# First pass of a batch in two steps of groups instead of three, and room for stacked tiles asked for later

## The chip, the cores and the metric

The kernel runs on one core of one Trainium2 chip. The metric is the device time of one execution in microseconds (us). Five engines work side by side, each through its own instructions in order: TensorE (PE, with its weight loads shown apart as PEld), VectorE (DVE), ScalarE (ACT), GpSimd (POOL) and SyncE (SP), which here only issues DMA transfers. They wait for one another by semaphores. A difference of about 0.2% (3 us) is what a measurement of this kernel can tell from no change.

## The reference, cut to what matters

```python
B, N, m, C = (4, 12480, 32, 128)
def mab(q, kv):
    s = scale * (q @ kv.transpose(0, 2, 1))
    s = s - s.max(-1, keepdims=True)
    a = np.exp(s)
    a /= a.sum(-1, keepdims=True) + 1e-09
    return a @ kv
h = mab(I, x)                       # 32 inducing rows look at the 12480 rows of a batch
x = mab(x, h).reshape(B * N, C)     # every row looks at the 32 rows of h
h = x @ w_in                        # 128 -> 2048
g = np.maximum(0.01 * h, h)
return g @ w_out                    # 2048 -> 128
```

All of it is float32. A batch therefore has a **first pass** (scores of the inducing rows against all rows, a softmax along 12480, the product with the rows: h), a **second pass** (scores of every row against h, a softmax along 32) and the two layers after it.

## The kernel before, in words

The last two layers are most of the work. The rows of all batches make 98 tiles, nearly all of 512 columns, and a tile goes through 16 **units**, one for each 128 of the 2048: 1568 units in all. A unit is four TensorE products of 512 columns and two evacuations: `ph` (line 712, the first layer, into PSUM), then on ACT `ghi` (line 725, the rectified value rounded to a short format) and on DVE `glo` (line 733, what the rounding left), then three products into `po` (line 751: ghi with w_hi, glo with w_hi, ghi with w_lo). At a tile's last unit one product more is added (line 770), and later DVE turns `po` into `osb` (line 780), which SP stores.

The products are written three units ahead (`LOOK = 3`): `ph` of unit u + 3 stands ahead of the `po` products of unit u. `ph` comes from the PSUM pool `ps_h`, which has three buffers. Helpers of the attention borrow from the same pool by `gen_ps`; other PSUM pools are `aux_ps` (two buffers), `ps_s` (one, tag `hp`) and `ps_o` (two, for `po`).

The attention of the next batch is woven into this stream. A loop over the units calls a few generators ("lanes"), and each call writes the next piece: `stores`, `stacking`, `seconds` (the softmax of the second pass for one group of rows), `scores` (`first_scores`) and `values` (`first_values`, then the weights for the next batch). A piece that costs DVE some 0.7 us yields `HEAVY` = 15; this debt is paid off by 4 a unit (5 in batch 0), and while there is debt the other lanes wait. So such pieces stand four units apart (three in batch 0).

The rows of a batch are 6 groups of 2048 and a remainder `RG` of 192. The first pass takes them in steps (`PASSES`) with a running maximum. At each step `first_scores` writes one **visit** of TensorE to the attention: the products of the step before with the rows (`value_products`), up to two second scores that the batch before still has to do (`waiting`, PSUM by `gen_ps`, each followed by its transpose on DVE, `turned`), and the first scores of the step's groups. Then `peaks` copies each group's scores out of PSUM into `e` on DVE and takes their maximum (line 282, called a peak below); it is the only reader of that PSUM buffer. One more visit brings the last value products, another the second scores that `expand_weights` starts with.

```python
ps_h = ctx.enter_context(tc.tile_pool(name="ps_h", bufs=LOOK, space=bass.MemoryType.PSUM))
def gen_ps(name):
    return ps_h.tile([P, TOK], F32, tag="ph", name=name)
```

`stack` makes the tiles `A4` that line 712 multiplies: ACT splits off `ahi` (line 641), POOL `alo` (line 646), both with one buffer, and SP copies them by DMA into `A4` (line 658), of which there are six.

Batch 0 has its first pass in an order written out by hand (`ORDER`), which the change does not touch; the weaving holds for the first passes of batches 1 to 3.

Of the kernel before, what the change touches and what calls it, by code (L numbers as in the profile page):

```python
# [20 lines left out]
def induced_attention_then_leaky_ffn(  # L21
# [24 lines left out]
    P = 128  # L46
# [81 lines left out]
    ring = set()  # L128
    PASSES = [[RG, 0, 1], [2, 3], [4, 5]]
    PASS_OF = {g: p for p, gs in enumerate(PASSES) for g in gs}  # L130
# [71 lines left out]
    def room(n=1):  # L202

        return not rows_live or rows_made[0] + n - 1 - min(i for i, _ in rows_live) < XR

# [63 lines left out]
    def peaks(b, p, sps):  # L269

        gs = PASSES[p]
        rm = sb.tile([P, len(gs)], F32, tag="rm", name="rm", bufs=2)
        if RG in gs:
            nc.vector.memset(rm[:, :1], -3.0e38)
        for i, g in enumerate(gs):
            _, J, K = GROUPS[g]
            w, rows = 32 * K, 32 * J
            if g == RG:
                e = sb.tile([P, w], F32, tag="er", name="er", bufs=1)
            else:  # L280
                e = sb.tile([P, TOK], F32, tag="e", name="e", bufs=2)
            nc.vector.tensor_scalar(  # L282
                out=e[:rows, :w],
                in0=sps[g][:rows, :w],
                scalar1=1.0,
                scalar2=None,
                op0=ALU.mult,
                op1=ALU.max,
                accum_out=rm[:rows, i : i + 1],
            )  # L290
            ex[b, g] = e
        return rm

    def running(b, p, rm):
        gs = PASSES[p]
        n = len(gs)
        nm_old = maxima.get(b)
        zg = sb.tile([P, 3], F32, tag="zg", name="zg", bufs=2)
# [3 lines left out]
        four = sb.tile([M, 12], F32, tag="rd", name="four", bufs=2)  # L302
        al = None
        for j in range(4):
            nc.gpsimd.tensor_scalar_mul(four[:, n * j : n * j + n], rm[32 * j : 32 * j + 32], -SCALE)
        yield
        if nm_old is None:
            nc.vector.tensor_reduce(out=nm[:M], in_=four[:, : 4 * n], op=ALU.min, axis=AX.X)
        else:
            least = sb.tile([M, 12], F32, tag="least", name="least", bufs=2)  # L310
# [12 lines left out]
        for i, g in enumerate(gs):  # L323
            _, J, K = GROUPS[g]
            w, rows = 32 * K, 32 * J
            e = ex[b, g]
            nc.scalar.activation(
                e[:rows, :w], e[:rows, :w], AF.Exp, bias=nm[:rows], scale=SCALE,
                accum_out=zg[:rows, i : i + 1],
            )  # L330
            yield
        zs = sb.tile([P, 1], F32, tag="zs", name="zs", bufs=2)
        nc.vector.tensor_reduce(out=zs, in_=zg[:, :n], op=ALU.add, axis=AX.X)
        if al is not None:
# [27 lines left out]
    def first_scores(b):  # L362


        halves = [(RG, 0, 3)] + [(g, j0, 2) for g in range(RG) for j0 in (0, 2)]
        blocks = {}
# [9 lines left out]
        for p, gs in enumerate(PASSES):  # L376
# [85 lines left out]
    def first_values(b):  # L462

        hacc = None
        for p, gs in enumerate(PASSES):
            while (b, p) not in summed:
                yield
            for g in gs:
# [3 lines left out]
                if g == RG:  # L472
                    ay = sb.tile([P, K, M], F32, tag="ayr", name="ayr", bufs=1)
                else:
                    ay = sb.tile([P, 16, M], F32, tag="ay", name="ay", bufs=2)
                nc.vector.transpose(ay[:rows, :K, :].rearrange("p k m -> p (k m)"), e[:rows, : 32 * K])
# [30 lines left out]
    def normalise(b, hacc, rz):  # L507

        same = e128.rearrange("p j m -> p (j m)")
        hs = sb.tile([P, C], F32, tag="hs", name="hs", bufs=1)  # L510
        nc.scalar.mul(hs, hacc, rz)
# [21 lines left out]
    def expand_weights(b):  # L533
# [4 lines left out]
        if b:  # L538
            while not room(2):
# [37 lines left out]
    def second(b, g, engines=None):  # L577
# [4 lines left out]
        rows, w = 32 * J, 32 * K  # L582
        if b == B - 1 and (b, g) not in early and g != RG and g > 1:
            while hw[b][2] is None or not room(len(waiting)):
# [43 lines left out]
    def stack(tiles_, engine=None):  # L628

        while len(A4) + len(tiles_) > A4_BUFS or not all(s[:2] in aT for t in tiles_ for s in t[1]):  # L630
            yield
# [11 lines left out]
        for (b, g), o in at.items():  # L643
# [192 lines left out]
    def start(stacking, seconds, chosen):  # L836
# [57 lines left out]
        def peak(g):  # L894
# [5 lines left out]
            if g == RG:  # L900
                e = sb.tile([P, TOK], F32, tag="e", name="e", bufs=2)
            else:
# [62 lines left out]
        def Y(g):  # L965
            J, K, rows, w = size(g)
            V["ay", g] = ay = sb.tile([P, 16, M], F32, tag="ay", name="ay", bufs=2)
            nc.vector.transpose(
# [35 lines left out]
        def gather(p):  # L1004
            hp = V.pop(("hp", p))[:, :C]
            if p == len(STEPS) - 1:
                V["hs"] = new = sb.tile([P, C], F32, tag="hs", name="hs", bufs=1)
                nc.vector.scalar_tensor_tensor(
# [20 lines left out]
        def scaled():  # L1029
            V["samez"] = r = sb.tile([P, P], F32, tag="samez", name="samez", bufs=1)  # L1030
            nc.scalar.mul(r, same, V["rz"])
# [76 lines left out]
        def first_second():  # L1108
# [3 lines left out]
            yield  # L1112
            y = sb.tile([P, 16, M], F32, tag="y", name="y", bufs=1)
            chosen["ysub"].tensor_tensor(
# [23 lines left out]
        def scales():  # L1138
            apart = sb.tile([P, 4, 16], F32, tag="apart", name="apart", bufs=1)
            nc.vector.tensor_tensor(  # L1140
# [10 lines left out]
        def scales_copy():  # L1151
            r = sb.tile([P, 4, 16], F32, tag="scr", name="scr", bufs=1)
            nc.scalar.copy(r.rearrange("p t k -> p (t k)"), V.pop("sc")[:, :64])
            token_scale.append(r)
# [45 lines left out]
        def second_turned(g):  # L1200
# [3 lines left out]
            if g:  # L1204
                y = sb.tile([P, 16, M], F32, tag="y", name="y", bufs=1)
                nc.vector.transpose(y.rearrange("p k m -> p (k m)"), V.pop(("s2", g)))
# [90 lines left out]
    with tc.manual_schedule():  # L1297
# [12 lines left out]
        for u in range(WOVEN, NT * NF):  # L1310
# [12 lines left out]
            if u >= 52 and u % 2:  # L1323
                step(fetches)
            if not debt[0]:
                step(seconds)
            if u >= max(due[0], 52) and not debt[0]:
                due[0] = u + (2 if b or u % 4 else 1)
                step(scores)
            if u >= 52 and (u >= due[1] or hw[max(hw)][2] is None) and not debt[0]:  # L1330
                due[1] = u + (2 if b or u % 4 else 1)
                known = len(hw)
                step(values)
                if len(hw) > known:
                    seconds += [second(known, g) for g in [0, 1, RG, 2, 3, 4, 5]]
        for gen in stores:
# [35 lines left out]
```

## Time and profile before

| what | value |
|---|---|
| median of 3 runs | 1491.11 us (1490.77 to 1491.75) |
| the profiled execution | 1490.82 us, span 1488.6 us |
| TensorE busy | 1477.5 us (99% of the span) |
| VectorE busy | 1262.6 us (85%) |
| ScalarE busy | 999.7 us (67%) |
| GpSimd busy | 116.7 us (8%) |
| granted TensorE clock | 0.999 |

The span runs from the first to the last instruction of the program; 2.2 us of the execution lie around it. The profile's matmul ends are modelled, and consecutive matmuls overlap in it, so the time of a stream is read from start to start.

### The profile page before, as it was taken

To read this page: it belongs to the slowest core of one execution; us is meant where nothing else is said; L and a number is where in the kernel's file an instruction comes from. 1 tells how busy PE (TensorE), PEld (TensorE's weight loads), DVE (VectorE), ACT (ScalarE), POOL (GpSimd) and SP (SyncE) were. 2 spreads that over 40 slices of the span, in tenths; PEclk is the share of its full clock that TensorE was granted. 3 is DMA by queue.
4 is the path that set the end of the run, shared out by engine and by line. 5 is a ranking of instruction groups with operands and counts; after the bars stand their busy time and mean duration, and the time that the engine had idled before them with its cause. 6 is when DMAs were issued, how large, how long until landed. Compare 5 with 4: busy or idle time off the path is not lost.

```text
span 1488.6 us, 22239 instructions
## 1 busy us (share of the span) xinstructions
PE 1477.5 (99%) x7861; PEld 1260.5 (85%) x7861; DVE 1262.6 (85%) x2129; ACT 999.7 (67%) x1749; POOL 116.7 (8%) x186
## 2 busy tenths in 40 slices
PE   9999999999999999999999999999999999999998
PEld 6788888888888888888888888888888898888887
DVE  6889889889898898889898898788888888888886
ACT  6766767666665766667675776676776666666665
POOL 1310101010100100010100100010100000000000
PEclk9999999999999999999999999999999999999999
DMA  8336355435444342343443440231212212212211
GB/s 286 67 81 119 53 89 118 93 66 97 92 89 82 95 92 51 55 89 67 91 88 69 110 92 16 48 71 21 46 36 40 43 22 50 43 22 50 40 25 22
DMA packets 402079, 105.23 MB, mean 71 GB/s; under 512 B 372624, under 2 KB 375088, under 8 KB 401968
## 3 DMA queue, kind: packets, MB, share of 16 engines
q1 hardware_dynamic: 401920, 103.80, 34.5%
q8 instruction: 62, 1.02, 0.3%
q14 instruction: 49, 0.40, 0.1%
q10 hardware_dynamic: 48, 0.02, 0.0%
HBM read 48.94 MB, written 25.56 MB: 50 GB/s over the span
## 4 chain that ended last, share of the span: by engine, by line
PE 98%; DMA 1%; DVE 0%; ACT 0%; issue 0%; SPq 0%; DVEq 0%; ACTq 0%
PE po L751 68%; PE ph L712 23%; PE s_ps L264 3%; PE po L770 1%; PE h_ps L440 1%; PE xT_ps L874 1%; DMA xr<-in_x_dram 0%; PE h_ps L995 0%; PE hw_ps L547 0%; PE w_ps L1095 0%; ACT ghi L725 0%; DMA hws<-hilo 0%; SPq L846 0%; PE winT_ps L1085 0%; DVE osb L780 0%
## 5 line engine op out<-in xcount | busy, mean ns | idle before, releaser
L725 ACT ACTIVATE ghi<-ph 128x512 fp32r<-128x512 f32 (+1 forms) x1568 | 929.3, 595 | 461.9 <-PE ph L712 456.3
L733 DVE SCALAR_TENSOR_TENSOR glo<-ph,ghi 128x512 fp32r<-128x512 f32 (+1 forms) x1568 | 1042.8, 679 | 183.0 <-ACT ghi L725 161.3
L712 PE MATMUL ph<-A,hws 128*128 128x512 f32 (+1 forms) x1600 | 594.9, 377 | 0.4 <-DMA hws<-hilo 0.3
L751 PE MATMUL po<-glo,w_hi 128*128 128x512 f32 (+1 forms) x1568 | 593.1, 378 | 1.2 <-DVE glo L733 1.2
L751 PE MATMUL po<-ghi,w_lo 128*128 128x512 f32 (+1 forms) x1568 | 593.0, 378 | 0.0
L751 PE MATMUL po<-ghi,w_hi 128*128 128x512 f32 (+1 forms) x1568 | 592.8, 379 | 0.0
L712 PEld LDWEIGHTS ph<-A,hws 128*128 128x128 f32 x1600 | 301.9, 189 | 58.1 <-DVE e L282 5.0
L751 PEld LDWEIGHTS po<-glo,w_hi 128*128 128x128 f32 x1568 | 296.4, 189 | 42.7 <-DVE glo L733 1.6
L751 PEld LDWEIGHTS po<-ghi,w_lo 128*128 128x128 f32 x1568 | 296.3, 189 | 41.2
L751 PEld LDWEIGHTS po<-ghi,w_hi 128*128 128x128 f32 x1568 | 296.4, 189 | 39.9 <-ACT ghi L725 0.2
L780 DVE STREAM_TRANSPOSE osb<-po 128x512 f32<-128x512 f32 (+1 forms) x98 | 68.9, 703 | 1.5 <-PE po L770 1.5
L646 POOL TENSOR_TENSOR alo<-aT,ahi 128x512 fp32r<-128x512 f32 x22 | 28.2, 1282 | 483.1 <-ACT ahi L641 463.2
L397 DVE STREAM_TRANSPOSE xT<-xc 128x512 f32<-128x512 f32 x72 | 50.5, 701 | 0.0
L599 POOL TENSOR_TENSOR y<-y,mx 128x512 f32<-128x512 f32 x23 | 24.2, 1052 | 243.6 <-DVE mx L597 219.1
L614 POOL TENSOR_TENSOR y<-y,sm 128x512 f32<-128x512 f32 x23 | 24.2, 1052 | 196.9 <-DVE sm L612 145.5
L770 PE MATMUL po<-A,m2s 128*128 128x512 f32 (+1 forms) x100 | 37.1, 374 | 0.0
L357 DVE STREAM_TRANSPOSE y<-s_ps 128x512 f32<-128x512 f32 x22 | 15.8, 717 | 10.9 <-PE s_ps L264 9.3
L264 PE MATMUL s_ps<-xT,hT 128*32 128x512 f32 x192 | 23.8, 596 | 0.4 <-ACT hT L1039 0.4
L264 PE MATMUL s_ps<-xT,indT 128*32 128x512 f32 x192 | 24.1, 595 | 0.0
L770 PEld LDWEIGHTS po<-A,m2s 128*128 128x128 f32 x100 | 18.9, 189 | 2.6
L282 DVE TENSOR_SCALAR_CACHE_REDUCE e<-s_ps 128x512 f32<-128x512 f32 x18 | 12.4, 690 | 8.0 <-PE s_ps L264 7.2
L440 PEld LDWEIGHTS h_ps<-xr,ay 128*32 128x32 f32 x576 | 15.2, 110 | 2.9 <-issue 2.6
(165 smaller groups left out, 376.1 us busy)
## 6 DMA issues: line engine op xcount, KB each, us to landing
xr<-in_x_dram SPq DMA_DIRECT2D x96, 256.0 KB, 4.4
out_dram<-osb SPq DMA_DIRECT2D x384, 64.0 KB, 2.2
xc<-in_x_dram SPq DMA_DIRECT2D x288, 64.0 KB, 2.8
A<-ahi SPq DMA_DIRECT2D x188, 64.0 KB, 2.0
A<-alo SPq DMA_DIRECT2D x188, 64.0 KB, 2.0
hws<-hilo SPq DMA_DIRECT2D x64, 64.0 KB, 2.0
raw<-in_moe_w_in_dram SPq DMA_DIRECT2D x4, 512.0 KB, 6.8
raw<-in_moe_w_out_dram SPq DMA_DIRECT2D x4, 512.0 KB, 10.3
```

The costliest lines, as they stand in the source:

```text
L264: nc.tensor.matmul(dst, lhsT, rhs, start=True, stop=True)
L397: nc.vector.transpose(t[:, j, :], blk.rearrange("p n c -> p (n c)"))
L440: nc.tensor.matmul(hp[32 * k : 32 * k + 32, :C], ay[:rows, 4 * q + k, :], xb[:rows, k, :], start=(i == 0 and q == 0), stop=(last[k] == i a ...
L599: engines[0].tensor_tensor(out=yv, in0=yv, in1=mx[:rows, :K].unsqueeze(2).broadcast_to([rows, K, M]), op=ALU.subtract,)
L614: engines[1].tensor_tensor(out=yv, in0=yv, in1=smv.unsqueeze(2).broadcast_to([rows, K, M]), op=ALU.mult)
L646: (engine or nc.gpsimd).tensor_tensor(out=alo[sl], in0=aT.pop((b, g))[: 32 * J, :], in1=ahi[sl].bitcast(F32), op=ALU.subtract,)
L712: nc.tensor.matmul(ph[:, o : o + w], hw[b][1][:, f * P : (f + 1) * P], woven(A4[t][:, o : o + w], t), start=True, stop=True,)
L725: nc.scalar.activation(halves(ghi[:, :n], t)[1], live[u][2], AF.Relu)
L733: nc.vector.scalar_tensor_tensor(out=halves(glo[:, :n], t)[1], in0=ph, scalar=0.0, in1=halves(ghi[:, :n], t)[1].bitcast(F32), op0=ALU.max, ...
L751: nc.tensor.matmul(accs[t][:, :n], w[:, f, :], woven(r[:, :n], t), start=(f == 0 and w is w_hi and r is live[u][0]), stop=False,)
L770: nc.tensor.matmul(accs[t][:, o : o + w], hw[b][2], woven(a4[:, o : o + w], t), start=False, stop=(o + w == n),)
L780: nc.vector.transpose(osb[:, :n], po[:, :n])
```

## The change

The first pass of batches 1 to 3 has two steps, groups 0, 1, 2 and then RG, 3, 4, 5. Their scores now lie in `aux_ps`, `aux_ps` and `hp` in the first step, and in `gen_ps` (RG), `aux_ps`, `aux_ps`, `gen_ps` (group 5) in the second. `peaks` yields `HEAVY` behind each group but the last. All waiting second scores (three now, since `expand_weights` does four groups itself) are written at once. The wait of `stack` for free `A4` buffers stands behind `ahi` and `alo`. The lanes that are called in a unit stop at the first debt, and `values` comes first while the next batch's weights are missing. Several SBUF tiles share tags, so that `e` and `ay` have three buffers.

```diff
-    PASSES = [[RG, 0, 1], [2, 3], [4, 5]]
+    PASSES = [[0, 1, 2], [RG, 3, 4, 5]]
...
-        return not rows_live or rows_made[0] + n - 1 - min(i for i, _ in rows_live) < XR
+        return len(rows_live) + n <= XR
...
-                e = sb.tile([P, TOK], F32, tag="e", name="e", bufs=2)
+                e = sb.tile([P, TOK], F32, tag="e", name="e", bufs=3)
...
             ex[b, g] = e
+            if i + 1 < len(gs):
+                yield HEAVY if g != RG else 0
         return rm
...
-            while b - 1 not in hw or hw[b - 1][2] is None or not room(min(2, len(waiting))):
+            while b - 1 not in hw or hw[b - 1][2] is None or not room(len(waiting)):
                 yield
...
-            for q in [waiting.pop(0) for _ in range(min(2, len(waiting)))]:
+            for q in [waiting.pop(0) for _ in range(len(waiting))]:
                 ps = gen_ps("s2_ps")
...
-                if g == RG:
+                if g == 2:
                     sps[g] = ps_s.tile([P, TOK], F32, tag="hp", name="s1_ps")
+                elif g in (RG, 5):
+                    sps[g] = gen_ps("s1_ps")
                 else:
                     sps[g] = aux_ps("s1_ps")
...
-            rm = peaks(b, p, sps)
+            rm = yield from peaks(b, p, sps)
...
-            for g, ps in [(RG, gen_ps("s2_ps")), (0, aux_ps("s2_ps")), (1, ps_s.tile([P, TOK], F32, tag="hp", name="s2_ps"))]:
+            for g in (RG, 2, 0, 1):
+                if g == 1:
+                    ps = ps_s.tile([P, TOK], F32, tag="hp", name="s2_ps")
+                else:
+                    ps = aux_ps("s2_ps") if g == 0 else gen_ps("s2_ps")
                 second_scores(b, g, ps)
                 turned(b, g, ps)
-            waiting.extend(range(2, RG))
+            waiting.extend(range(3, RG))
...
-        while len(A4) + len(tiles_) > A4_BUFS or not all(s[:2] in aT for t in tiles_ for s in t[1]):
+        while not all(s[:2] in aT for t in tiles_ for s in t[1]):
             yield
...
         yield
+        while len(A4) + len(tiles_) > A4_BUFS:
+            yield
         for t, parts in tiles_:
...
-            if not debt[0]:
-                step(seconds)
-            if u >= max(due[0], 52) and not debt[0]:
+            urgent = hw[max(hw)][2] is None
+            for lane in (values, seconds, scores) if urgent else (seconds, scores, values):
+                if debt[0]:
+                    break
```

TensorE carries out the same matmuls before and now. What moves is best seen at the visit of the second step of batch 1. On TensorE before, the visit ends with one second score (`s2_ps`, from `gen_ps`) and the first scores of groups 2 and 3 (`s1_ps`, both from `aux_ps`):

```order
L440 MATMUL h_ps_2960<-xr_1438,ayr_2420 32x128 x2
L264 MATMUL s2_ps_2995<-xT_409,hT_653 32x512 x4
L264 MATMUL s1_ps_3002<-xT_2443,indT_82 32x512 x4
L264 MATMUL s1_ps_3007<-xT_2674,indT_82 32x512 x4
L712 MATMUL ph_3017<-A4_1975,hws_675 128x512
L751 MATMUL po_2867<-ghi_2935,w_hi_79 128x512
```

On TensorE now it ends with RG (`s1_ps_3549`, from `gen_ps`), groups 3 and 4 (`aux_ps`) and group 5 (`s1_ps_3563`, from `gen_ps`):

```order
L444 MATMUL h_ps_3500<-xr_1945,ay_3453 32x128 x4
L264 MATMUL s1_ps_3549<-xTr_2697,indT_82 32x64 x3
L264 MATMUL s1_ps_3553<-xT_2773,indT_82 32x512 x4
L264 MATMUL s1_ps_3558<-xT_3003,indT_82 32x512 x4
L264 MATMUL s1_ps_3563<-xT_3223,indT_82 32x512 x4
L722 MATMUL ph_3574<-A4_2691,hws_675 128x512
L761 MATMUL po_3372<-ghi_3475,w_hi_79 128x512
```

So two buffers of the pool of `ph` are taken by first scores, which before had none of that pool.

On DVE before, at the same place, the transpose of the second score and both peaks follow one another between two `glo`:

```order
L733 SCALAR_TENSOR_TENSOR glo_2955<-ph_2951,ghi_2953 128x512
L357 STREAM_TRANSPOSE y_3000<-s2_ps_2995 128x512
L282 TENSOR_SCALAR e_3013,rm_3012<-s1_ps_3002 128x512
L282 TENSOR_SCALAR e_3015,rm_3012<-s1_ps_3007 128x512
L733 SCALAR_TENSOR_TENSOR glo_3021<-ph_3017,ghi_3019 128x512
```

On DVE now the peaks of RG and group 3 stand first, two `glo` apart; three `glo` on come the peak of group 4 and what follows here, up to that of group 5:

```order
L282 TENSOR_SCALAR e_3625,rm_3568<-s1_ps_3558 128x512
L743 SCALAR_TENSOR_TENSOR glo_3631<-ph_3627,ghi_3629 128x512
L743 SCALAR_TENSOR_TENSOR glo_3642<-ph_3638,ghi_3640 128x512
L743 SCALAR_TENSOR_TENSOR glo_3654<-ph_3650,ghi_3652 128x512
L790 STREAM_TRANSPOSE osb_3659<-po_3372 128x512
L743 SCALAR_TENSOR_TENSOR glo_3666<-ph_3662,ghi_3664 128x512
L743 SCALAR_TENSOR_TENSOR glo_3675<-ph_3671,ghi_3673 128x512
L743 SCALAR_TENSOR_TENSOR glo_3686<-ph_3682,ghi_3684 128x512
L282 TENSOR_SCALAR e_3695,rm_3568<-s1_ps_3563 128x512
L743 SCALAR_TENSOR_TENSOR glo_3701<-ph_3697,ghi_3699 128x512
```

From the visit to the peak of group 5, the only reader of `s1_ps_3563`, there are now 11 `glo`; in batch 2 there are 26 and in batch 3 there are 17. The other DVE instructions of the 0.7 us kind ahead of that last peak are: in batch 1 two peaks and one `osb`; in batch 2 two peaks, two `osb`, one `aT` and one `mx`; in batch 3 two peaks, one `osb` and one `aT`.

On ACT the splits for the tile that batches 0 and 1 share (`ahi<-aTr`, twice) are followed by the next split after 19 `ghi` now:

```order
L649 CAST ahi<-aTr 96x64 x2
L735 ACTIVATE ghi<-ph 128x512 x3
L329 ACTIVATE e,zg<-e,nm 128x512
L735 ACTIVATE ghi<-ph 128x512 x5
L329 ACTIVATE e,zg<-e,nm 128x512
L735 ACTIVATE ghi<-ph 128x512 x9
L613 ACTIVATE y<-y 128x512
L735 ACTIVATE ghi<-ph 128x512 x2
L649 CAST ahi<-aT 128x512
```

Before, 59 `ghi` stood between the two.

## Rows read from the trace of the kernel before

**Rows 1.** The page: busy us by engine, and the chain that ended last.
```profile
PE 1477.5 (99%) x7861; PEld 1260.5 (85%) x7861; DVE 1262.6 (85%) x2129; ACT 999.7 (67%) x1749; POOL 116.7 (8%) x186
...
PE 98%; DMA 1%; DVE 0%; ACT 0%; issue 0%; SPq 0%; DVEq 0%; ACTq 0%
```

**Rows 2.** The view of waits, PE alone: us in total, times, longest.
```profile
PE po L751 <- DVE glo L733: 1.2, 1, 1.2
...
PE ph L712 <- DMA hws<-hilo: 0.3, 1, 0.3
```

**Rows 3.** Busy us by stretch: PE, PEld, DVE, ACT, POOL; then clock, DMA.
```profile
0.00:50.00 50.00, 46.10 (x482) 31.46 (x483) 35.76 (x100) 33.21 (x67) 9.95 (x13) 1.00 0.70 230
...
446.00:600.00 154.00, 154.00 (x892) 132.88 (x895) 132.93 (x226) 102.40 (x182) 11.51 (x25) 1.00 0.38 78
```

**Rows 4.** Timeline at 432 us, plain units: start, us, engine, instruction [idle before].
```profile
432.65 0.38 PE L712 MATMUL ph<-A,hws 128*128 128x512 f32 x1
...
433.06 0.60 ACT L725 ACTIVATE ghi<-ph 128x512 fp32r<-128x512 f32 x1 [0.27 <-PE ph L712]
...
433.51 0.38 PE L712 MATMUL ph<-A,hws 128*128 128x512 f32 x1
...
433.69 0.69 DVE L733 SCALAR_TENSOR_TENSOR glo<-ph,ghi 128x512 fp32r<-128x512 f32 x1 [0.17 <-ACT ghi L725]
...
434.30 0.68 DVE L609 TENSOR_REDUCE sm<-y 128x16 f32<-128x512 f32 x1
...
434.89 0.70 DVE L397 STREAM_TRANSPOSE xT<-xc 128x512 f32<-128x512 f32 x1
...
435.52 2.55 DVE L733 SCALAR_TENSOR_TENSOR glo<-ph,ghi 128x512 fp32r<-128x512 f32 x4
...
435.89 0.38 PE L751 MATMUL po<-ghi,w_lo 128*128 128x512 f32 x1
436.23 0.19 PEld L712 LDWEIGHTS ph<-A,hws 128*128 128x128 f32 x1 [0.37 <-DVE glo L733]
...
436.55 0.38 PE L751 MATMUL po<-ghi,w_hi 128*128 128x512 f32 x1
...
436.75 0.60 ACT L725 ACTIVATE ghi<-ph 128x512 fp32r<-128x512 f32 x1 [0.50 <-PE ph L712]
```

**Rows 5.** Timeline at 383 us: the visit of the first step of batch 2.
```profile
383.42 0.69 DVE L733 SCALAR_TENSOR_TENSOR glo<-ph,ghi 128x512 fp32r<-128x512 f32 x1 [0.17 <-ACT ghi L725]
...
383.88 0.38 PE L751 MATMUL po<-ghi,w_lo 128*128 128x512 f32 x1
...
384.19 0.16 PEld L264 LDWEIGHTS s_ps<-xT,hT 128*32 128x32 f32 x8 [0.33 <-DVE glo L733]
...
384.28 0.69 DVE L733 SCALAR_TENSOR_TENSOR glo<-ph,ghi 128x512 fp32r<-128x512 f32 x1 [0.17 <-ACT ghi L725]
384.65 0.13 PEld L264 LDWEIGHTS s_ps<-xT,hT 128*32 128x32 f32 x4 [0.30 <-issue]
...
387.20 0.68 DVE L282 TENSOR_SCALAR_CACHE_REDUCE e<-s_ps 128x512 f32<-128x512 f32 x1
...
387.87 0.48 PE L712 MATMUL ph<-A,hws 128*128 128x512 f32 x1
...
388.01 0.69 DVE L282 TENSOR_SCALAR_CACHE_REDUCE e<-s_ps 128x512 f32<-128x512 f32 x1
388.19 0.38 PE L751 MATMUL po<-ghi,w_hi 128*128 128x512 f32 x1
```

**Rows 6.** Groups of DVE instructions, shapes apart: busy us, mean ns of one, idle before.
```profile
L733 DVE SCALAR_TENSOR_TENSOR glo<-ph,ghi 128x512 fp32r<-128x512 f32 x1536 | 1025.7, 682 | 178.9 <-ACT ghi L725 157.2
L780 DVE STREAM_TRANSPOSE osb<-po 128x512 f32<-128x512 f32 x96 | 67.8, 706 | 1.5 <-PE po L770 1.5
...
L623 DVE STREAM_TRANSPOSE aT<-y 128x512 f32<-128x512 f32 x23 | 16.1, 700 | 0.0
```

**Rows 7.** SP's timeline: first and last of the shared tile's 24 transfers.
```profile
403.69 0.56 SPq L658 DMA_DIRECT2D A<-ahi  x1
...
418.23 0.59 SPq L658 DMA_DIRECT2D A<-alo  x1
```

**Rows 8.** The view of DMA: such transfers, KB each, median us to landing.
```profile
A<-ahi SPq DMA_DIRECT2D x24, 8.0 KB, 1.7
```

More of the change, by code (lines that the diff above doesn't have):

```diff
@@ L297, in running @@
         nm_old = maxima.get(b)
-        zg = sb.tile([P, 3], F32, tag="zg", name="zg", bufs=2)
+        zg = sb.tile([P, 4], F32, tag="zg", name="zg", bufs=2)
         if RG in gs:
@@ L301, in running @@
         nm = sb.tile([P, 1], F32, tag="nm", name="nm", bufs=3)
-        four = sb.tile([M, 12], F32, tag="rd", name="four", bufs=2)
+        four = sb.tile([M, 16], F32, tag="rd", name="four", bufs=2)
         al = None
@@ L309, in running @@
         else:
-            least = sb.tile([M, 12], F32, tag="least", name="least", bufs=2)
+            least = sb.tile([M, 16], F32, tag="least", name="least", bufs=2)
             nc.vector.tensor_scalar(
@@ L362, in first_scores @@
     def first_scores(b):
-        halves = [(RG, 0, 3)] + [(g, j0, 2) for g in range(RG) for j0 in (0, 2)]
+        halves = [h for gs in PASSES for g in gs for h in ([(RG, 0, 3)] if g == RG else [(g, 0, 2), (g, 2, 2)])]
         blocks = {}
@@ L474, in first_values @@
                 else:
-                    ay = sb.tile([P, 16, M], F32, tag="ay", name="ay", bufs=2)
+                    ay = sb.tile([P, 16, M], F32, tag="ay", name="ay", bufs=3)
                 nc.vector.transpose(ay[:rows, :K, :].rearrange("p k m -> p (k m)"), e[:rows, : 32 * K])
@@ L509, in normalise @@
         same = e128.rearrange("p j m -> p (j m)")
-        hs = sb.tile([P, C], F32, tag="hs", name="hs", bufs=1)
+        hs = sb.tile([P, C], F32, tag="hacc", name="hs", bufs=2)
         nc.scalar.mul(hs, hacc, rz)
@@ L538, in expand_weights @@
         if b:
-            while not room(2):
+            while not room(3):
                 yield
-            for g, ps in [(RG, gen_ps("s2_ps")), (0, aux_ps("s2_ps")), (1, ps_s.tile([P, TOK], F32, tag="hp", name="s2_ps"))]:
+            for g in (RG, 2, 0, 1):
[3 more added lines that the diff above has]
+                    ps = aux_ps("s2_ps") if g == 0 else gen_ps("s2_ps")
                 second_scores(b, g, ps)
                 turned(b, g, ps)
-            waiting.extend(range(2, RG))
+            waiting.extend(range(3, RG))
         pw = aux_ps("hw_ps")
@@ L582, in second @@
         rows, w = 32 * J, 32 * K
-        if b == B - 1 and (b, g) not in early and g != RG and g > 1:
+        if b == B - 1 and (b, g) not in early and g != RG and g > 2:
             while hw[b][2] is None or not room(len(waiting)):
@@ L900, in peak @@
             if g == RG:
-                e = sb.tile([P, TOK], F32, tag="e", name="e", bufs=2)
+                e = sb.tile([P, TOK], F32, tag="e", name="e", bufs=3)
             else:
@@ L966, in Y @@
             J, K, rows, w = size(g)
-            V["ay", g] = ay = sb.tile([P, 16, M], F32, tag="ay", name="ay", bufs=2)
+            V["ay", g] = ay = sb.tile([P, 16, M], F32, tag="ay", name="ay", bufs=3)
             nc.vector.transpose(
@@ L1006, in gather @@
             if p == len(STEPS) - 1:
-                V["hs"] = new = sb.tile([P, C], F32, tag="hs", name="hs", bufs=1)
+                V["hs"] = new = sb.tile([P, C], F32, tag="hacc", name="hs", bufs=2)
                 nc.vector.scalar_tensor_tensor(
@@ L1029, in scaled @@
         def scaled():
-            V["samez"] = r = sb.tile([P, P], F32, tag="samez", name="samez", bufs=1)
+            V["samez"] = r = sb.tile([P, P], F32, tag="m2s", name="samez", bufs=2)
             nc.scalar.mul(r, same, V["rz"])
@@ L1112, in first_second @@
             yield
-            y = sb.tile([P, 16, M], F32, tag="y", name="y", bufs=1)
+            y = sb.tile([P, 16, M], F32, tag="e", name="y", bufs=3)
             chosen["ysub"].tensor_tensor(
@@ L1138, in scales @@
         def scales():
-            apart = sb.tile([P, 4, 16], F32, tag="apart", name="apart", bufs=1)
+            apart = sb.tile([P, 4, 16], F32, tag="er", name="apart", bufs=1)
             nc.vector.tensor_tensor(
@@ L1151, in scales_copy @@
         def scales_copy():
-            r = sb.tile([P, 4, 16], F32, tag="scr", name="scr", bufs=1)
+            r = sb.tile([P, 4, 16], F32, tag="ayr", name="scr", bufs=1)
             nc.scalar.copy(r.rearrange("p t k -> p (t k)"), V.pop("sc")[:, :64])
@@ L1204, in second_turned @@
             if g:
-                y = sb.tile([P, 16, M], F32, tag="y", name="y", bufs=1)
+                y = sb.tile([P, 16, M], F32, tag="e", name="y", bufs=3)
                 nc.vector.transpose(y.rearrange("p k m -> p (k m)"), V.pop(("s2", g)))
@@ L1324, in induced_attention_then_leaky_ffn @@
                 step(fetches)
-            if not debt[0]:
-                step(seconds)
-            if u >= max(due[0], 52) and not debt[0]:
[L1328 to L1335, printed above, removed]
+            urgent = hw[max(hw)][2] is None
+            for lane in (values, seconds, scores) if urgent else (seconds, scores, values):
+                if debt[0]:
+                    break
+                if lane is seconds:
+                    step(seconds)
+                elif lane is scores:
+                    if u >= max(due[0], 52):
+                        due[0] = u + (2 if b or u % 4 else 1)
+                        step(scores)
+                elif u >= 52 and (u >= due[1] or urgent):
+                    due[1] = u + (2 if b or u % 4 else 1)
+                    known = len(hw)
+                    step(values)
+                    if len(hw) > known:
+                        seconds += [second(known, g) for g in [0, 1, RG, 2, 3, 4, 5]]
         for gen in stores:
```

## The prediction

> **What bounds the kernel now.** I read the page first, then the view of waits, the stretches, and the timeline at single places. On the page TensorE is busy 99% of the span and 98% of the chain that ended last is TensorE's [rows 1]. Busy time of overlapping matmuls says little, so look at the starts: in plain units `ph` follows `ph` after 0.86 us (432.65, 433.51), four products of 0.216 us with nothing between [rows 4]. TensorE's whole wait for `glo` is 1.2 us and `ph`'s for a transfer 0.3 us [rows 2]; a stretch of 154 us is filled by it [rows 3]. So TensorE is the bound, it has no idle time to give back, and whatever makes it wait is added to the end. The other engines may be late only by their lead over it, and the change matters where it shortens that lead.
>
> How long is the lead? `ph` starts at 432.65, ACT's `ghi` 0.41 later (433.06), DVE's `glo` 0.63 after that (433.69), which takes 0.69 [rows 4]. From the end of a `glo` to the weight load that waits for its buffer are 0.08 us (383.42 + 0.69, then 384.19) [rows 5]. A `ph` that waited starts in effect 0.10 us behind its weight load: 436.23 to 436.55 is 0.32 where one product takes 0.216 [rows 4]. So a PSUM buffer of `ph` can be used again 0.41 + 0.63 + 0.69 + 0.08 + 0.10 = 1.91 us later. With three buffers this may take three units, 2.59 us, which leaves 0.68 us.
>
> The trace has a test of this. At 434.30 and 434.89 two DVE operations of 0.68 and 0.70 us stand between two `glo`, and the next `glo` starts at 435.52 instead of 433.69 + 0.86 = 434.55, 0.97 late [rows 4]. By the sum 0.97 - 0.68 = 0.29 us should reach TensorE. It shows 0.23: the product at 436.55 was due at 435.89 + 2 x 0.216 = 436.32. A single such operation stays hidden; two together do not.
>
> **The change part by part.**
>
> *Fewer visits.* TensorE's matmuls are the same. Each visit breaks the stream twice: into it, 383.88 to 384.19 is 0.31 where 0.216 is usual, and out of it 387.87 to 388.19 is 0.32 [rows 5], 0.2 us in all. One visit less in each of three batches gives -0.6 us.
>
> *Three second scores at once.* The third takes the buffer of the last `ph` ahead of the visit, whose `glo` ends at 384.28 + 0.69 = 384.97 and frees it at 385.05. Weight loads of a visit are 0.46 apart (384.19, 384.65), so even with one of these steps per score the third could not start before 385.11 [rows 5]: no wait. Their transposes lie beside the first scores of the same visit.
>
> *Room later, smaller DVE and POOL work, lane order.* `ph` hardly waits for a stacked tile (0.3 us, and that for `hws`) [rows 2], so earlier `ahi` and `alo` give nothing. The dropped maxima and sums are hidden by TensorE. I take 0 for both; if the cover were gone, they would give back at most the 1.2 us of waits for `glo`.
>
> *Group 5's scores in the pool of `ph`.* This is the term that decides. The buffer of `s1_ps_3563` is free only when its peak has run, and DVE works in order: 11 `glo` stand ahead of that peak in batch 1, 26 in batch 2, 17 in batch 3. RG's buffer comes back at once, its peak being first. So for 54 units `ph` has two buffers: it waits for the `glo` of two units back, and the lead of 0.68 us becomes 1.73 - 1.91 = -0.18.
>
> Take a DVE operation of length H between the `glo` of units u and u + 1. With two buffers `ph` of u + 3 waits for that second `glo`. From `ph` of u: 0.41 + 0.63 to the first `glo`, 0.69, H, 0.69, then 0.08 + 0.10: 2.60 + H, for three units that TensorE does in 2.59. So H falls wholly on TensorE. With three buffers it is `ph` of u + 4 that waits, with 3.46 us to spend, and H of 0.7 to 0.8 fits; that is why the same operations cost nothing now. They stand three or four units apart, so each pays for itself: the next chain begins where the last has ended.
>
> Their lengths: a peak 0.81, from 387.20 to the next start at 388.01 with its reading of the accumulator [rows 5]; `osb` 0.71, `aT` 0.70 [rows 6]; `mx` as the reduction of the same shape, 0.68 [rows 4]. Batch 1: 2 x 0.81 + 0.71 = 2.33. Batch 2: 2 x 0.81 + 2 x 0.71 + 0.70 + 0.68 = 4.42. Batch 3: 2 x 0.81 + 0.71 + 0.70 = 3.03. Behind the last operation of each stretch one loop of two units without help costs 0.18, three times 0.5. Together +10.3 us for 13 operations and 54 units.
>
> No row of before shows two buffers, so bounds: below, the pair at 434 cost 0.23 us, and 13 times that is 3.0; above, if the 0.18 of every two units came on top of H, 54 x 0.09 = 4.9 more, 15.2. I take 10.3, since the chain was right within 0.06 us in the test.
>
> A rule of the Trainium skill would make it smaller. The row shows that it is the weight load of `ph` itself that waits for DVE, 0.37 us (436.23) [rows 4], and the 0.10 us behind it are in my chain. "TensorE: Matmul & The Clock Gate", section "Architectural detail: the array is 16× 32×32, not 1× 128×128", says that TensorE's queue can pull weight loads ahead of matmuls in flight. If that held for a load whose matmul waits, the 0.10 would go from each of 13 chains, and 10.3 would become 9.0. The trace does not agree at this place, and I stay with the row.
>
> **The sum.** -0.6 + 10.3 = +9.7 us. On the profiled execution, 1490.82 with its span of 1488.6 and 2.2 around it, that is 1500.5; that execution is 0.3 below the median, so for the median 1491.11 + 9.7 = **1500.8 us**, 0.65% slower.
>
> **The rivals.**
>
> *A, the pool isn't short.* The peak would come early, or the lead would suffice, and the saved visits remain: 1491.1 - 0.6 = 1490.5, no change that can be told; with the waits for `glo` gone as well, 1489.3. For it: in the 50 us of the hand-written start, DVE and ACT are behind TensorE too and all goes well. Against it: the one reader of the buffer stands where the order shows it. It decides if the cost of an operation is under about 0.25 us, three us in all. Chance 0.10, of which 0.03 faster.
>
> *B, half of it is hidden.* A long visit of TensorE (384.19 to 387.87, 3.7 us) [rows 5] lets DVE run ahead, and the first operations might be paid from this: half of 10.3, 1495.7. Against it: the lead can't exceed what two buffers hold. Chance 0.10.
>
> *C, a further wait on ACT.* `ahi` has one buffer. The 24 transfers of the shared tile take from 403.69 to 418.23, 14.5 us [rows 7], and land in 1.7 [rows 8], 16.2 in all, while the next `ahi` now comes after 19 `ghi`, 19 x 0.86 = 16.4 (59 before). If SP is some us late there, ACT stands, and all beyond 0.68 us reaches TensorE, in two places: 1 to 2 us each, 1503.8. Against it: it just fits, and POOL and SP are mostly idle. Chance 0.13.
>
> *D, the clock falls.* The stalls would come at every few units, and TensorE's granted clock could drop from the 2.4 GHz level to 1.2 in the 54 units: each would take 0.86 us more, 47 in all, 1537. Against it: in the first 50 us TensorE is busy 46.10 only, and its granted clock there is 1.00 [rows 3]. The same page of the Trainium skill, section "A second HAM failure mode: psum-queue depth-cycling", describes this: matmul groups that cycle through PSUM banks with short idle times make the clock go to and fro. By that rule the rival comes true; no trace here has shown it. Chance 0.02.
>
> **How the numbers follow.** The forecast holds 0.65 of the chance. Its own range, by the bounds, is 1493.5 to 1505.7; B and C lie inside it or at its ends. A and D, 0.12, stay out, and I cut the ends a little: 1495 to 1505. A change under 0.2%, 3 us, can't be told from none with this kernel. Slower: forecast, C, D and most of B, 0.89. Same: most of A and a little of B, 0.08. Faster: 0.03.
>
> **What the profile of the changed kernel would show.** Right: TensorE's wait of `ph` (now line 722) for `glo` rises from about 1 us to some 10, in three stretches of about 11, 26 and 17 units behind the visits of the second steps, each with a stall two units behind every DVE operation of 0.7 us, and nearly none elsewhere. The 1.5 us of other waits stay, and the granted clock stays at 1.00. Wrong: stalls at each `ph` of these stretches of 0.18 per pair alone (the operations hidden), waits of ACT for DMA, or `ph` at 0.86 us throughout, which would be A.

## The result, and the profile after

The changed kernel takes 1501.9 us (median of 6 runs, 1501.46 to 1503.7), the kernel before beside it 1491.0 us (6 runs, 1490.31 to 1491.75): ratio 1.0077, 95% interval 1.0066 to 1.0087. It is slower by 10.9 us, where the forecast was 9.7 slower and 1500.8 us. The total was right, but the trace shows that it is made of other parts than the forecast's. Ratios below are to the kernel before, run beside each kernel on the same chip; where two changed versions are compared, it is by their medians. The trace of the changed kernel is of the slowest of the six executions (1503.7).

The page of the changed kernel, busy time and the chain that ended last, answers to [rows 1]. TensorE is still the bound. Its busy time rose by 10.1 us with the same matmuls: short stalls hide there under the modelled ends (0.38 us for a product that starts every 0.216), and a short stretch at a lower clock, shown below, adds to it.
```profile
PE 1487.6 (99%) x7861; PEld 1259.5 (84%) x7861; DVE 1259.8 (84%) x2114; ACT 998.6 (66%) x1746; POOL 112.8 (8%) x165
...
PE 97%; DVE 1%; ACT 1%; DMA 0%; issue 0%; SPq 0%; POOL 0%; DVEq 0%; ACTq 0%; POOLq 0%
```

The view of waits of the changed kernel (us in total, times, longest): of matmuls, of their weight loads (PEld) and of ACT. The first line answers to [rows 2].
```profile
PE ph L722 <- DVE glo L743: 4.3, 2, 3.5
...
PEld ph L722 <- DVE glo L743: 22.3, 54, 3.9
...
ACT ahi L649 <- DMA A<-alo: 4.1, 1, 4.1
```

The second line is the best single measure here, because a `ph` that lacks a PSUM buffer shows it at its weight load. Before, the same line was this, which the view of PE alone in [rows 2] does not show:
```profile
PEld ph L712 <- DVE glo L733: 4.4, 16, 0.5
```

The third line above is new: before, ACT never waited at `ahi` for a transfer.

**The stretches in which group 5's scores hold a buffer** (the hold, below). The same view for the weight loads, in three windows (270 to 290, 566 to 600, 925 to 955 us) behind the visits of the second steps:
```profile
PEld ph L722 <- DVE glo L743: 2.4, 7, 0.5
...
PEld ph L722 <- DVE glo L743: 4.7, 13, 0.5
...
PEld ph L722 <- DVE glo L743: 3.2, 9, 0.5
```

That is 10.3 us of waiting in 29 waits (equal to the forecast's term by accident: it is not what TensorE loses). What it loses is read from the timeline at 566 us (start, us, engine, instruction, idle before), to be held against [rows 4]:
```profile
565.59 0.38 PE L722 MATMUL ph<-A,hws 128*128 128x512 f32 x1
...
566.24 0.38 PE L761 MATMUL po<-ghi,w_lo 128*128 128x512 f32 x1
566.52 0.19 PEld L722 LDWEIGHTS ph<-A,hws 128*128 128x128 f32 x1 [0.30 <-DVE glo L743]
...
566.64 0.69 DVE L743 SCALAR_TENSOR_TENSOR glo<-ph,ghi 128x512 fp32r<-128x512 f32 x1 [0.17 <-ACT ghi L735]
566.84 0.38 PE L761 MATMUL po<-ghi,w_hi 128*128 128x512 f32 x1
...
567.24 0.71 DVE L790 STREAM_TRANSPOSE osb<-po 128x512 f32<-128x512 f32 x1
...
567.87 1.35 DVE L743 SCALAR_TENSOR_TENSOR glo<-ph,ghi 128x512 fp32r<-128x512 f32 x2
...
568.13 0.38 PE L761 MATMUL po<-ghi,w_lo 128*128 128x512 f32 x1
568.58 0.19 PEld L722 LDWEIGHTS ph<-A,hws 128*128 128x128 f32 x1 [0.47 <-DVE glo L743]
...
568.90 0.38 PE L761 MATMUL po<-ghi,w_hi 128*128 128x512 f32 x1
...
570.79 0.38 PE L761 MATMUL po<-ghi,w_hi 128*128 128x512 f32 x1
```

Two products after 568.13 the stream should be at 568.56, and it is at 568.90: 0.34 lost with a wait of 0.47. Two after 566.24 it should be at 566.67 and is at 566.84: 0.17 lost with a wait of 0.30. So a wait costs its length less 0.13, and 29 of them cost 10.3 - 29 x 0.13 = 6.5 us. The whole round of four units with one DVE operation takes 570.79 - 566.84 = 3.95 us where four units take 3.46: 0.49 for the operation, and 13 of them give 6.4.

**A stall that the forecast had at nothing.** Timeline of SP, ACT and PE of the changed kernel from 459 to 479 us, with the two `ahi` of the same stretch as the view of that tile lists them (count, durations, first and last start):
```profile
459.51 5.62 SPq L250 DMA_DIRECT2D xc<-in_x_dram  x8
465.24 0.58 SPq L668 DMA_DIRECT2D A<-ahi  x1
...
475.34 0.59 SPq L668 DMA_DIRECT2D A<-alo  x1
...
477.45 0.62 ACT L649 CAST ahi<-aT 128x512 fp32r<-128x512 f32 x1 [4.14 <-DMA A<-alo]
...
479.11 0.74 PE L722 MATMUL ph<-A,hws 128*128 128x192 f32 x2 [3.54 <-DVE glo L743]
...
L649 ACT CAST ahi<-aT x2: 609/614/618, 453.4 to 477.5; 128x512 fp32r<-128x512 f32 x2
```

The `ahi` written at 453.4 is copied only from 465.24 on: its transfers are now written behind the wait for room, and on SP they stand behind the eight loads of `xc`, while `ahi` itself no longer waits. The last of them is issued at 475.34. `ahi` has one buffer, so the next one, which ACT has reached at 477.45 - 4.14 = 473.31, stands there until the last copy has landed, with every `ghi` behind it. TensorE's lead takes up the first 0.60 us of these 4.14, and it stands the other 3.54. The windows around it (PE, PEld, DVE, ACT, POOL busy; clock, DMA share, GB/s) show a second price:
```profile
470.00:477.00 7.00, 5.56 (x37) 5.22 (x35) 3.50 (x7) 1.97 (x4) 0.00 (x0) 1.00 0.53 131
477.00:479.50 2.50, 0.39 (x2) 0.39 (x3) 1.00 (x3) 1.77 (x4) 1.28 (x1) 0.67 0.79 213
479.50:486.00 6.50, 6.50 (x29) 6.50 (x29) 4.09 (x9) 2.54 (x6) 0.00 (x0) 0.60 0.67 106
486.00:500.00 14.00, 14.00 (x70) 12.52 (x69) 12.56 (x21) 9.89 (x17) 1.06 (x1) 1.00 0.43 66
```

Behind the stall the granted clock is 0.60 for 6.5 us, and TensorE does 29 matmuls there. The median does not show in how many executions this happens.

**Smaller ones.** At 194 us three DVE operations now stand together, the middle one short, after three of ACT that come with one `ghi` each between (188.94, 190.13, 191.31); one weight load waits 1.12 us (timeline of the changed kernel):
```profile
193.07 0.67 DVE L617 TENSOR_REDUCE sm<-y 128x16 f32<-128x512 f32 x1
...
193.72 0.70 DVE L480 STREAM_TRANSPOSE ay<-e 128x512 f32<-128x512 f32 x1
...
195.05 0.19 PEld L722 LDWEIGHTS ph<-A,hws 128*128 128x128 f32 x1 [1.12 <-DVE glo L743]
```

### The profile page after: what moved, and what is told of

Read it like the earlier page. It is cut to its first block, busy times and chain, and to the rows that moved or that the text cites. A ratio compares the mean times of both kernels' runs of the same rounds, so it can differ in the third digit from the quotient of the medians.

```text
span 1501.9 us, 22206 instructions
## 1 busy us (share of the span) xinstructions
PE 1487.6 (99%) x7861; PEld 1259.5 (84%) x7861; DVE 1259.8 (84%) x2114; ACT 998.6 (66%) x1746; POOL 112.8 (8%) x165
## 4 chain that ended last, share of the span: by engine, by line
PE 97%; DVE 1%; ACT 1%; DMA 0%; issue 0%; SPq 0%; POOL 0%; DVEq 0%; ACTq 0%; POOLq 0%
PE po L761 66%; PE ph L722 23%; PE s_ps L264 3%; PE po L780 1%; PE h_ps L444 1%; PE xT_ps L884 1%; DVE glo L743 1%; ACT ghi L735 0%; PE h_ps L1005 0%; PE warm_ps L1246 0%; PE hw_ps L555 0%; PE w_ps L1105 0%; SPq L668 0%; DVE osb L790 0%; DMA xr<-in_x_dram 0%
## 5 line engine op out<-in xcount | busy, mean ns | idle before, releaser
L722 PEld LDWEIGHTS ph<-A,hws 128*128 128x128 f32 x1600 | 302.8, 190 | 73.5 <-DVE glo L743 22.3
L649 ACT CAST ahi<-aT 128x512 fp32r<-128x512 f32 x23 | 14.1, 612 | 6.1 <-DMA A<-alo 4.1
```

The source lines that it names most:

```text
L722: nc.tensor.matmul(ph[:, o : o + w], hw[b][1][:, f * P : (f + 1) * P], woven(A4[t][:, o : o + w], t), start=True, stop=True,)
```

## The experiments

The theory after this reading: the hold costs some 6 us and not 10, the later wait for room some 3.5, and the order of the lanes (which pieces now meet in one unit) 1 to 2. The rival: the hold costs what was forecast, and the stall at 477 us is paid back later or is an accident of one execution. By the intervals, a difference between two medians of this table is uncertain by some 2 us. The last column is the view of waits of the whole run, weight loads of `ph` for `glo`, us and times.

| kernel | median us (range, runs) | ratio to before, 95% | `ph` <- `glo` |
|---|---|---|---|
| before | 1491.0 to 1491.24, beside the others | | 4.4, 16 |
| changed | 1501.9 (1501.46 to 1503.7, 6) | 1.0077, 1.0066 to 1.0087 | 22.3, 54 |
| e1_short_hold | 1497.23 (1495.75 to 1498.89, 5) | 1.0040, 1.0028 to 1.0053 | 14.4, 34 |
| e2_room_first | 1498.41 (1498.08 to 1499.59, 5) | 1.0050, 1.0037 to 1.0062 | 17.8, 51 |
| e3_both | 1494.15 (1493.44 to 1495.16, 11) | 1.0020, 1.0011 to 1.0029 | 10.5, 30 |
| e4_room_late_alone | 1494.66 (1492.87 to 1496.81, 11) | 1.0023, 1.0014 to 1.0032 | 8.7, 19 |
| e5_two_held | 1536.48 (one run) | | 55.9, 70 |
| e6_peaks_together | 1494.95 (1492.69 to 1498.41, 9) | 1.0032, 1.0022 to 1.0041 | 9.2, 26 |
| e7_both_adjacent | 1492.45 (1491.51 to 1493.95, 11) | 1.0010, 1.0001 to 1.0019 | 7.7, 23 |
| e8_pairs_apart | 1491.62 (1490.11 to 1492.91, 11) | 1.0005, 0.9996 to 1.0014 | 6.3, 19 |
| e9_bunch_apart | 1492.04 (1490.4 to 1494.12, 11) | 1.0007, 0.9998 to 1.0016 | 5.3, 19 |
| e10_before_pairs | 1492.36 (1491.6 to 1493.38, 11) | 1.0010, 1.0001 to 1.0019 | 6.3, 21 |

### e1_short_hold: the pool's buffer goes to group 3 instead of group 5

```diff
-                elif g in (RG, 5):
+                elif g in (RG, 3):
                     sps[g] = gen_ps("s1_ps")
```

TensorE's visit is as long, but the buffer's reader is now the second peak and not the last.

> The changed kernel, but in the second step the scores of group 3 instead of group 5 lie in the pool of ph (group 5's lie in aux_ps); every engine's order stays as it is. Theory H (a score kept in the pool of ph leaves ph two buffers, and each DVE operation of the 0.7 us kind that runs meanwhile costs TensorE 0.4 to 0.5 us): the peak of group 3 comes early, 17 units instead of 54 and 3 operations instead of 13 are left, so 4 to 5 us less than the changed kernel, about 1497. Theory V (the larger visits themselves cost, the buffer does not matter): no change, 1502. The wait of ahi for transfers near 477 us and the lower clock behind it stay.

Measured: 1497.23 us, 4.7 less than the changed kernel, and 20 waits less for `glo`. The stall at ACT stays, as these lines of its waits and windows show:
```profile
ACT ahi L649 <- DMA A<-alo: 3.4, 1, 3.4
```
```profile
470.00:477.00 7.00, 4.21 (x29) 3.89 (x28) 3.09 (x7) 3.09 (x7) 1.09 (x1) 1.00 0.59 162
477.00:479.50 2.50, 2.50 (x18) 2.50 (x19) 2.37 (x6) 1.48 (x3) 0.18 (x1) 1.00 0.86 159
479.50:486.00 6.50, 6.50 (x38) 6.18 (x38) 5.89 (x11) 4.46 (x8) 1.05 (x1) 1.00 0.60 95
```

So how long the buffer is held sets a cost, and it is 4.7 us for the longer part of it. The trace agrees: in windows that take in the three stretches (270 to 290, 560 to 606, 915 to 965 us) 9 of the 29 waits are left, with 3.2 of the 10.3 us, and 7.1 less 20 x 0.13 is 4.5. The clock does not fall here; in 479.5 to 486 us TensorE does 38 matmuls, 9 more than in the changed kernel, at 6.5 / 38 = 0.17 us each. So the slower clock cost the changed kernel's traced execution some 1.5 us.

### e2_room_first: the stack waits for room ahead of its splits again

```diff
-        while not all(s[:2] in aT for t in tiles_ for s in t[1]):
+        while len(A4) + len(tiles_) > A4_BUFS or not all(s[:2] in aT for t in tiles_ for s in t[1]):
             yield
...
-        while len(A4) + len(tiles_) > A4_BUFS:
-            yield
```

> The changed kernel, but stack waits for room in A4 ahead of ahi and alo again, as before the change. Theory R (asked for early, ahi stands on ACT behind transfers that SP has not issued yet, and that costs 3.7 us at one place and about 2 us more by the clock that falls behind it): the wait of ahi for A4's transfers is gone, and 4 to 6 us less than the changed kernel, 1496 to 1498, with the granted clock at 1.00 throughout. If the wait is only moved to another instruction on ACT: 1502 as the changed kernel. The stalls of the second steps stay at about 6 us.

Measured: 1498.41 us, 3.5 less than the changed kernel. ACT has no wait at `ahi` for a transfer any more, and in the windows named at e1 all 29 waits stay, with the same 10.3 us. The stall at 477 us was neither hidden nor given back. Its trace has a granted clock of 1.00 there (465 to 490 us), but not throughout, as was expected: it is 0.66 from 10 to 15 us, in the start that no edit touches, behind an idle time of TensorE of 1.33 us.

### e3_both: e1 and e2 together

> Both edits of the two runs before it. If H and R are the whole cause and independent: 9 to 11 us less than the changed kernel, 1491 to 1493, the time of the kernel before, with one to two us left from three DVE operations in short holds and from the stall at 194 us. If they share a cause, or something else costs too: clearly above 1493.

Measured: 1494.15 us, 7.75 below the changed kernel, where the two single savings add to 4.7 + 3.5 = 8.2. They are separate costs, as far as the noise can tell. 3.0 us (1.6 to 4.3 by the interval) over the kernel before are left.

### e4_room_late_alone: the kernel before, with only the wait for room moved behind the splits

```diff
-        while len(A4) + len(tiles_) > A4_BUFS or not all(s[:2] in aT for t in tiles_ for s in t[1]):
+        while not all(s[:2] in aT for t in tiles_ for s in t[1]):
             yield
...
+        while len(A4) + len(tiles_) > A4_BUFS:
+            yield
         for t, parts in tiles_:
```

> The kernel before, with the wait for room of stack moved behind ahi and alo and nothing else. If late room is harmful by itself: a wait of ahi for A4's transfers of some us, 1493 to 1497. If it needs the two-step first pass beside it (its transfers crowd SP at that place only with it): no such wait, within 1 us of 1491.

Measured: 1494.66 us, ratio 1.0023 (1.0014 to 1.0032), 3.4 us slower. The moved wait is harmful without the rest of the change, and at another place, right behind the shared tile. Its waits, its timeline there and one window:
```profile
ACT ahi L641 <- DMA A<-ahi: 4.8, 3, 2.7
```
```profile
415.16 0.59 SPq L660 DMA_DIRECT2D A<-alo  x1
...
416.32 0.62 ACT L641 CAST ahi<-aT 128x512 fp32r<-128x512 f32 x1 [2.73 <-DMA A<-ahi]
...
418.21 0.80 PE L714 MATMUL ph<-A,hws 128*128 128x512 f32 x1 [2.02 <-DVE glo L735]
```
```profile
418.00:422.00 4.00, 3.79 (x10) 3.10 (x11) 3.16 (x7) 1.60 (x3) 1.35 (x2) 0.57 1.03 280
```

The transfer issued at 415.16 is the last of the shared tile's 24. This is the mechanism of rival C at the place that it named, with 2.0 us at TensorE and a slow clock (0.57) behind it.

### e5_two_held: groups 4 and 5 in the pool of `ph`

```diff
-                elif g in (RG, 5):
+                elif g in (4, 5):
```

> The changed kernel, but in the second step groups 4 and 5 lie in the pool of ph (RG and 3 in aux_ps); the order of every engine stays. Until the peak of group 4 there is one buffer left for ph (36 units), from there to the peak of group 5 two (18 units). Theory H: with one buffer a unit takes the whole loop of 1.91 us where TensorE needs 0.86, so about 1.05 x 36 = 38 us more, less the part of the stalls of the changed kernel that lies in these units (about 4): 1535 to 1545, more if the granted clock falls there. If the buffers of ph do not matter: 1502.

Measured: 1536.48 us, 34.6 above the changed kernel, with 55.9 us of waits. Where one buffer is left, the whole chain of ACT and DVE is on the path. Two windows of it:
```profile
560.00:600.00 40.00, 27.98 (x212) 18.09 (x210) 18.13 (x33) 12.49 (x21) 2.10 (x2) 1.00 0.29 62
...
940.00:975.00 35.00, 25.05 (x200) 16.18 (x200) 15.31 (x29) 10.75 (x18) 0.00 (x0) 1.00 0.27 64
```

TensorE is busy 70% and 72% there, with idle times of at most 0.8 us again and again, and its granted clock stays at 1.00. In these windows the time is that of waiting alone. This kernel too has one stall behind ACT's wait at `ahi`, of 2.78 us, and the granted clock falls behind that one, as this window shows:
```profile
484.00:490.00 6.00, 6.00 (x23) 6.00 (x23) 3.60 (x8) 1.96 (x4) 0.00 (x0) 0.50 0.69 118
```

### e6_peaks_together: the changed kernel without the debt between the peaks

```diff
-            if i + 1 < len(gs):
-                yield HEAVY if g != RG else 0
+        yield from ()
```

> The changed kernel, but peaks takes all groups of a step at once, without HEAVY between them; group 5 stays in the pool of ph. Theory H: it is the distance in time to the peak of group 5 that costs, so the stalls of the three second steps (about 6 us) go, although the pool is shared as before; 1495 to 1497, as the run with group 3 in the pool or a little better. Rival: it is the borrowing itself, or four peaks in a row (3.2 us on DVE) make a new wait of TensorE as long as the old ones: 1500 or more. The wait of ahi for transfers may stay or move, since room is still asked for late.

Measured: 1494.95 us, 7.0 less than the changed kernel, with the scores in the same PSUM buffers. Where the peaks stand at once behind the visit, the weight loads have no wait for `glo` in the three windows. So it is not the borrowing of a buffer that costs, but the time until its reader has run. The waits at ACT are shorter but not gone (view of waits):
```profile
ACT ahi L648 <- DMA A<-ahi: 1.9, 2, 1.7
```

### e7_both_adjacent: e3, and `peaks` no longer yields behind RG

```diff
-            if i + 1 < len(gs):
-                yield HEAVY if g != RG else 0
+            if g != RG and i + 1 < len(gs):
+                yield HEAVY
```

The peak of group 3 then follows that of RG at once, so its buffer is free right behind the visit.

> The run with both edits, and the peak of group 3 straight behind that of RG, so that no score stays in the pool of ph at all. Theory H: the last 1.5 us of stalls in the second steps of batches 2 and 3 go, 1492.5 to 1493; what is left above the kernel before then is DVE and ACT operations that the new lane order puts together (0.2 to 1 us each, at 195, 350, 400 us and later). Rival: these stalls come from something else: 1494 as the run with both edits.

Measured: 1492.45 us, 1.7 below e3, and the 9 waits that e1 left are gone. With e1's 4.7 the hold is worth 6.4 us by medians, as 13 x 0.49 from the timeline.

### e8_pairs_apart and e9_bunch_apart: what the order of the lanes costs

e8 is e7 with a debt behind the sum `sm` of a second score; e9 has it in batch 1 too, and a call of its own for each exponential.

```diff
-        yield
+        yield 5 if b > 1 else 0
```
```diff
-        yield 5 if b > 1 else 0
+        yield 5 if b else 0
...
+            yield
```

> The kernel of the run before it (both edits, peaks adjacent), and the sum of the second pass (0.68 us on DVE, which yields no debt) yields 5 in batches 2 and 3, so that no transpose follows it in the same unit. If the 0.23 us stalls at such pairs are what is left: three of them go, 0.7 us less than the run before it, about 1492; if lane order in general costs: no difference.

> The version of e8_pairs_apart, with the sum of a second score also paying debt in batch 1, and each exponential of the running maximum in a call of its own. What is left in e8_pairs_apart over the pace of before is the stall of 0.9 us at 194 us (three ACT operations nearly together, then three DVE operations one behind another) and a few of 0.23 us in batch 1 where a sum and a transpose meet. Theory that these are all that is left: both go, 1.0 to 1.5 us less than e8_pairs_apart, 1490 to 1490.6, ratio to the kernel before 0.9993 to 1.0000. Rival, that the stall at 194 us comes from a transfer or from something else than the meeting of these operations: it stays, 1491.2 to 1491.8.

Measured: 1491.62 and 1492.04 us. The trace went as the theory said: the waits of weight loads for `glo` fall from 7.7 us (e7) to 6.3 and 5.3 us, the longest from 1.1 to 0.4, and the wait at 194 us is gone in e9. The time did not: e9 is not below e8. In e9's trace TensorE waits more for the rows of x, in the view of waits:
```profile
PE xT_ps L883 <- DMA xr<-in_x_dram: 1.4, 3, 0.6
...
PE h_ps L445 <- DMA xr<-in_x_dram: 1.2, 2, 0.6
```

Before, the first of these is 0.7 us and the second is not there, which makes 1.9 us of e9's longer span (1490.9 against 1488.6). The first stands in the start; the second stands at the last value products of batch 1, between 320 and 345 us, and e8 and the changed kernel do not have it. Why these rows come late was not tried. Neither kernel beats the kernel before, and neither can be told from it.

### e10_before_pairs: the kernel before, with debt behind the sum

```diff
-        yield
+        yield HEAVY
```

> The kernel before, with the sum of a second score followed by the debt of a heavy piece. Theory that a sum and a transpose of x in one unit cost 0.23 us each, whatever the kernel: such pairs stand four times in the kernel before, so it gains at most 0.9 us, 1490.2 to 1491, and the stall at 436 us is gone from the trace. Rival, that the stall at 436 us has another cause: the trace still shows a weight load of the first layer waiting 0.37 us there.

Measured: 1492.36 us, ratio 1.0010 (1.0001 to 1.0019); the gain did not come. The wait at 436 us is gone, but weight loads wait 21 times, 6.3 us, against 16 times, 4.4 us. In the trace of the kernel before, a sum of 0.7 us with a transpose right behind it stands seven times (the expectation counted four), in e10 never; but other operations now meet, such as an `osb` behind a late `glo` at 258 us. So what a pair costs is shown by its stall, but an edit of the debt cannot be priced by the pairs that it removes.

## Why the prediction was right, and where its steps were not

The forecast +9.7 and the measured +10.9 are this close by luck: the main term was right in kind and too large, and what was taken as 0 made up for it. By the prediction's own signs, the stalls in three stretches came as forecast, but a wait of ACT for DMA, which it named as a sign of being wrong, came too, and the granted clock did not stay at 1.00. The parts, in us:

| part | forecast | measured |
|---|---|---|
| group 5's scores in the pool of `ph` | +10.3 | +6.4 (e1 and e7: 4.7 + 1.7) |
| room later | 0 | +3.1 to +3.5 (e1 to e3, changed to e2, e4 to before) |
| lane order and fewer visits together | -0.6 | +1.5 (e7 to before, interval 0.1 to 2.8) |

**The hold: mechanism right, term mis-sized.** The buffer of group 5 stays until the last peak, three stretches of `ph` with two buffers follow, and DVE's operations reach TensorE there: the trace, e1, e6 and e7 show each link. The step that failed is "So H falls wholly on TensorE", with the lengths H taken from the durations. The chain of the forecast is 2.60 + 0.71 = 3.31 for an `osb`; from 565.59 to the start in effect 568.90 - 0.22 = 568.68 it took 3.09. The missing 0.22 are in three links: `glo` to `osb` 0.60 (566.64, 567.24) instead of 0.69, `osb` to `glo` 0.63 instead of 0.71, `glo` to the weight load 0.71 (567.87, 568.58) instead of 0.77 (`ghi`, 0.01 later, takes back the rounding). On a DVE that works without a break the next operation starts before the row of the last one ends. [Rows 4] had it: 434.30, 434.89, 435.52 are 0.59 and 0.63 apart, with durations of 0.68 and 0.70, and the weight load at 436.23 stands 0.71 behind the start of its `glo`. The forecast used these rows to test its chain and took the difference of 0.06 as agreement; with starts instead of durations it would have been 13 x 0.5. The Trainium skill, "Perfetto Trace Analysis", section "DVE / Act Engine Instruction (TENSOR_ADD, Activation, etc)", says that a profiled duration runs to the acknowledgement of the write while the next instruction may begin its prefetch before it; this trace agrees in that the rows overlap, by 0.07 to 0.09 us each.

**Room later: the step that failed is "I take 0 for both".** It asked what an earlier `ahi` could give and not what it could take. The splits now run ahead of their transfers, and the one buffer of `ahi` is then full for longer: the 20 us from the `ahi` at 453.4 to the time when ACT reached the next (473.31) were not enough, because the transfers began 12 us late. Rival C had this mechanism, its size per place (1 to 2 us, measured 2.0 to 3.5) and a chance of 0.13, but only for the place behind the shared tile. There its own count "it just fits" held in the changed kernel, where the `ahi` at 453.4 has no wait for a transfer, and failed in e4.

**Lane order.** The forecast took its cost as 0. The bunch at 194 us and further pairs show as stalls, but e9 and e10 could not price them, so of the last line of the table only the sum is known, and its cause stays open. The -0.6 for visits is not shown by itself.

**Rivals.** A, that the pool isn't short, is ruled out by the 29 waits in the three stretches. B has nearly the size of the hold (half of 10.3), but its reason, a lead won in the visit, is not what the trace shows: the `osb` at 567.24, two `glo` behind the visit, already costs 0.34. D did not come: in the windows 270 to 290, 566 to 600 and 925 to 955 us of the changed kernel the granted clock is 1.00, the 2.4 GHz level, and e5 with much more idle time holds it in the two windows shown. The clock did fall, but behind single longer stalls, which D did not name. The rule of the Trainium skill beside it ("TensorE: Matmul & The Clock Gate", "A second HAM failure mode: psum-queue depth-cycling") does not agree with e5's two windows. The other rule that the prediction cites from the Trainium skill, weight loads pulled ahead, gives nothing where a `ph` waits: there the load itself stands, 0.30 and 0.47 us.

## What to carry to other kernels

In this kernel a PSUM buffer borrowed from a pool in a tight loop cost by the time until its last reader had run, and nothing that showed where the reader came at once: put that reader first, or give the borrowed buffer to the piece that is read first. A wait moved behind the writing of a staging buffer holds that buffer, and the next writer's engine with it, so count its buffers before you take an earlier start as free. Build chains of an engine that is never idle from starts of rows, not from their durations.

## What the runs showed of the hardware that was not expected

In the changed kernel one idle time of TensorE of 3.5 us was followed by 6.5 us at a granted clock of 0.60 (near the 1.2 GHz level), in e5 one of 2.8 us by 6 us at 0.50, and in e4 one of 2.0 us by 4 us at 0.57. In e1 one of 2.8 us left the clock at 1.00, and so did e5's 40 us with 12 us idle in pieces of at most 0.8 us. The length of one idle time alone does not decide, as e1 and e5 show with the same length; what does was not found.
